# Attention with a relative bias and a squared-relu FFN on one core: the order of every engine's instructions taken from a list scheduler

## The chip, the cores and the metric

The kernel runs on one core of a Trainium2 chip. The metric is the device time of one execution in microseconds (us), the median over several runs. A core has five engines that each work through a list of instructions in order: TensorE (PE in the profile, with its weight loads shown apart as PEld), VectorE (DVE), ScalarE (ACT), GpSimd (POOL, which here issues DMAs and sets memory) and SyncE (SP, which here issues DMAs). An engine waits at an instruction until what it reads has been written and what it writes over has been read; instructions behind it on the same engine wait with it.

## The reference

The inputs are q, k and v with 8 batches, 8 heads, 576 positions and 64 values a head, a bias table of 32 buckets by 8 heads, and FFN weights of 512 x 2048 and 2048 x 512, all fp32. What is computed:

```
scores = scale * np.matmul(q, k.transpose(0, 1, 3, 2))
bias = bias_table[bucket]                  # bucket depends on |i - j| alone
scores = scores + bias.transpose(2, 0, 1)[None, :, :, :]
attn = np.exp(scores - max); attn = attn / (attn.sum + 1e-09)
x = (attn @ v), heads side by side         # 4608 tokens x 512
h = np.maximum(x @ w_in, 0.0)
out = h * h @ w_out                        # 4608 x 512, fp32
```

## The kernel before

The work is cut into 64 *units*. A unit is one pair of heads (two heads side by side fill 128 partitions) with half of a batch's queries, 288 of them. Four units, one a pair of heads, make a *half* h (16 of them, two a batch): 288 tokens with all eight heads, which the FFN can then take.

A unit has five score steps jt over blocks of 128 keys (the fifth has the 64 last keys of both heads). Each is one or two matmuls (`scores`, L264 and L280) into one of two PSUM buffers `st`, an exp on ACT into `et` or `em` (L273, L282), and, where the block touches the band in which the bias changes, a multiply on DVE by the exponentiated bias table `tb_sb` or `tm_sb` (L288). Outside the band the bias is a constant, which drops out in the quotient. Then `pv` (L318) multiplies by v, whose tile `vz` also holds columns of ones, so that the same matmul gives the row sums; each head's result has one PSUM bank. ACT takes Ln of both sums and Exp of minus that (L325, L326, L329), and two multiplies on DVE write the normalised result to `xt` (L335).

For a half that is complete, `ffn1` makes 16 groups of four matmuls (L362) into one PSUM bank `f1` (`hps`), each followed by a relu on ACT into `rt` (L371) and a square on DVE into `g_sb` (L372). `ffn2` makes, per 128 tokens, 16 matmuls of 512 columns (L384) into one bank `f2` (`yps`), a scaled copy on DVE (L390) and a store from SP. `ffn1` of a half needs all eight `xt` multiplies of that half.

q and k must lie transposed. For batches 0 and 1 PE does that (`transposes`, L233, into `f1` or `f2`) and DVE copies the result into `kz` (L250 to L252) and `qt` (L246). From batch 2 on, POOL's DMAs write fp16 copies of q and k to DRAM (`halve`), SP's transposing DMAs read them back (`turn`, L157), and DVE spreads k (L160 to L162).

The bias table is made on the chip at the start: exp of the table's differences, one matmul with a constant, a copy on DVE (L202), one DMA to DRAM (`t_bias`) and five DMAs back, in which each partition reads the row shifted by one. All six are on SP. The loads of q, k, v and the weights are on POOL.

What sets the order is written out by hand. `run(h)` lists the slots of a half: score steps, transposes, and the two parts of the `pv` of the unit before at fixed places. After every slot it calls `feed`, which emits `ffn1` groups and pairs of `ffn2` matmuls that are due by a clock of its own: a half lasts STEP = 28 ticks, spread evenly over its slots, `ffn1` of a half begins 9 ticks after the half, and `ffn2` begins at a tick in the third half after it. `defer` and `tick` put the Exp and the two multiplies one slot apart. After the last slot, `alone = True`: the groups of `ffn1` that are left use `f1` and the two `pv` banks by turns, and `ffn2` the score buffers.

Of the kernel before, what the change touches and what calls it, by code (L numbers as in the profile page):

```python
# [21 lines left out]
NBK = 32  # L22
# [8 lines left out]


STEP, AFTER1, AFTER2 = 28, 9, 3

F2_GAP = 4.0

DMA_FROM = 2
F2_PACE = STEP * 16 / 288
F2_START = 5 * STEP + AFTER1 + AFTER2 - 48 * F2_PACE
TILES = [(0, 1), (2, 3), (4, 5), (6, 7, 8)]  # L40
BAND = [(0, 256), (0, 384), (128, 512), (256, 576), (384, 576)]


def _bucket(n):
# [7 lines left out]
    return np.where(n < half, n, large).astype(np.int64)  # L52


@with_exitstack
def kernel(
# [30 lines left out]
    et_pool = ctx.enter_context(tc.tile_pool(name="et", bufs=11))  # L87
    nr_pool = ctx.enter_context(tc.tile_pool(name="nr", bufs=2))
    kt_pool = ctx.enter_context(tc.tile_pool(name="kt", bufs=2))
    em_pool = ctx.enter_context(tc.tile_pool(name="em", bufs=3))  # L90
    xt_pool = ctx.enter_context(tc.tile_pool(name="xt", bufs=2))
    rt_pool = ctx.enter_context(tc.tile_pool(name="rt", bufs=3))
# [22 lines left out]


    def sdma(eng, out_, in_):
        io(eng.dma_start(out=out_, in_=in_))  # L118

    qts, spreads = {}, []  # L120

    def load_qk(b, h0, n):

        for dst, src in zip(h16s[b], (q, k)):
            sdma(
                nc.gpsimd,
                dst[:, h0 : h0 + n, :],
                src[b, h0 : h0 + n].rearrange("h (p t) d -> p h (t d)", t=TPP),
            )

    def halve(b):

        for ic in range(2):
            sdma(
                nc.gpsimd,
                bass.AP(
                    tensor=d16[0],
                    offset=(b * S + ic * IC) * H * D,
                    ap=[[D, H], [H * D, IC], [1, D]],
                ),  # L140
                bass.AP(
                    tensor=q.tensor,
                    offset=q.offset + (b * H * S + (ic + 1) * IC - 1) * D,
                    ap=[[S * D, H], [-D, IC], [1, D]],
                ),
            )
        for h in range(H):
            sdma(nc.gpsimd, d16[1].ap()[b, :, ts(h, D)], k[b, h])

    def turn(p):  # L150

        b, hp = divmod(p, 4)
        qt = qt_pool.tile([128, S], FP16, tag="qt", name="qt")
        kz = kzs[p % 5]
        kt = kt_pool.tile([128, S], FP16, tag="kt", name="kt")
        for out_, src in ((qt, d16[0]), (kt, d16[1])):
            io(nc.sync.dma_start_transpose(out=out_, in_=src.ap()[b, :, ts(hp, 128)]))  # L157
# [424 lines left out]
```

## Time and profile before

| what | value |
|---|---|
| time, median of 3 runs (lowest, highest) | 473.96 us (473.86, 474.88) |
| the profiled execution's own time | 472.76 us |
| its span, first to last instruction | 470.9 us |
| mean clock granted to TensorE | 0.976 |
| PE, ACT, DVE, POOL busy | 429.9, 338.2, 271.5, 125.3 us |
| first `hps` matmul, first `yps` matmul begin at | 42.0, 77.5 us |
| last scores' exp ends, last `yps` matmul begins | 427.4, 466.3 us |
| DMA moved | 36.58 MB |

The profile is one execution. A row of a group names the line, the engine, the operation and the tiles, with its count, its busy time and the mean of one; behind the second bar stands how long the engine was idle just before and what ended that. A row of the timeline has start, length, engine, line and count, and in square brackets the idle time before it and its releaser. A row of waits has the total, the number and the longest. Since matmuls overlap, a busy PE is not a PE at its peak.

### The profile page before, as it was taken

How to read it: one execution, taken by the hardware profiler on the slowest of the kernel's cores; microseconds unless marked ns; L12 is line 12 of the kernel's file. 1: busy time of each engine (PE TensorE's matmuls, PEld its weight loads, DVE VectorE, ACT ScalarE, POOL GpSimd, SP SyncE). 2: the span in 40 equal slices, each digit the busy share in tenths (PEclk: the TensorE clock that was granted, in tenths of full speed). 3: DMA queues.
4: the chain of work that ended last, by engine and by line, in shares of the span. 5: the costliest groups of instructions: out<-in, count | busy, mean ns of one | idle time of the engine just before them, and what ended most of it. 6: DMA issues, size and time to landing. Idle time of an engine off the chain costs nothing.

```text
span 470.9 us, 8483 instructions
## 1 busy us (share of the span) xinstructions
PE 429.9 (91%) x3023; PEld 282.5 (60%) x3023; DVE 271.5 (58%) x790; ACT 338.2 (72%) x770; POOL 125.3 (27%) x169
## 2 busy tenths in 40 slices
PE   6477988999999999999999999999999999996996
PEld 2244656666666666666666666666666666663552
DVE  5768955565555755556556655565556655553331
ACT  2287888787778877787778877787778877784330
POOL 7948285003800084003800084003200000000000
PEclk9599999999999999999999999999999999998899
DMA  9999999543994289344994189433514200000011
GB/s 125 205 200 129 149 98 95 70 86 44 90 112 67 61 73 119 75 62 56 92 112 75 53 71 120 75 69 48 52 49 61 61 24 24 22 24 23 24 45 67
DMA packets 165801, 36.58 MB, mean 78 GB/s; under 512 B 152920, under 2 KB 161152, under 8 KB 165760
## 3 DMA queue, kind: packets, MB, share of 16 engines
q0 software_dynamic: 129504, 18.47, 53.7%
q1 hardware_dynamic: 36256, 17.59, 16.0%
q8 instruction: 23, 0.38, 0.4%
q14 instruction: 18, 0.15, 0.1%
HBM read 37.75 MB, written 16.52 MB: 115 GB/s over the span
## 4 chain that ended last, share of the span: by engine, by line
PE 78%; ACT 10%; DVE 6%; issue 3%; DMA 3%; SPq 0%; DVEq 0%
PE yps L384 26%; PE hps L362 24%; PE pv L318 14%; PE st L264 12%; ACT et L273 4%; ACT rt L371 2%; ACT r L326 2%; ACT r L325 1%; DMA t_bias<-tv_sb 1%; PE st L280 1%; DVE xt L335 1%; DMA tb_sb<-t_bias 1%; DVE kz L251 1%; DVE kz L250 1%; DVE y L390 1%
## 5 line engine op out<-in xcount | busy, mean ns | idle before, releaser
L273 ACT ACTIVATE et<-st 128x576 f16<-128x576 f32 x256 | 164.1, 645 | 24.1 <-PE st L264 22.6
L362 PE MATMUL hps<-xt,w_in_sb 128*128 128x288 f16 x1024 | 168.1, 287 | 5.4 <-ACT rt L371 3.5
L384 PE MATMUL yps<-w_out_sb,g_sb 128*128 128x512 f16 x576 | 167.1, 381 | 0.6 <-DVE y L390 0.6
L371 ACT ACTIVATE rt<-hps 128x288 f16<-128x288 f32 x256 | 104.6, 409 | 80.5 <-PE hps L362 80.3
L288 DVE TENSOR_TENSOR et<-et,tb_sb 128x512 f16<-128x512 f16 (+3 forms) x224 | 79.2, 356 | 111.3 <-ACT et L273 105.2
L362 PEld LDWEIGHTS <-w_in_sb 128*128 128x128 f16 x1024 | 100.2, 98 | 55.1 <-issue 6.7
L264 PE MATMUL st<-qt,kz 128*128 128x288 f16 x512 | 104.8, 288 | 18.3 <-ACT et L273 14.7
L372 DVE TENSOR_TENSOR g_sb<-rt 128x288 f16<-128x288 f16 x256 | 78.5, 307 | 58.9 <-ACT rt L371 55.7
L118 POOL DMA_DIRECT2D vz<-in_v_dram x80 | 57.9, 739 | 174.7 <-PE pv L318 163.1
L318 PE MATMUL pv<-et,vz 128*128 128x288 f16 x512 | 84.6, 289 | 1.0 <-DVE xt L335 1.0
L264 PEld LDWEIGHTS <-kz 128*128 128x128 f16 x512 | 49.7, 98 | 58.7 <-issue 27.1
L318 PEld LDWEIGHTS <-vz 128*128 128x128 f16 x640 | 62.7, 99 | 26.6 <-DVE xt L335 1.4
L384 PEld LDWEIGHTS <-g_sb 128*128 128x128 f16 x576 | 56.6, 98 | 22.4 <-issue 1.7
L335 DVE TENSOR_TENSOR xt<-pv,r 64x288 f16<-64x288 f32 x128 | 58.0, 453 | 4.7 <-ACT r L329 1.9
L118 POOL DMA_DIRECT2D k<-in_k_dram x48 | 30.9, 680 | 31.1 <-DMA q<-in_q_dram 23.6
L318 PE MATMUL pv<-em,vz 128*128 128x288 f16 x128 | 36.9, 288 | 1.1 <-DVE em L288 1.1
L390 DVE TENSOR_SCALAR y<-yps 128x512 f32<-128x512 f32 x36 | 24.9, 692 | 11.7 <-PE yps L384 11.0
L329 ACT ACTIVATE r<-r 128x288 f32<-128x288 f32 x64 | 28.3, 443 | 2.0
L325 ACT ACTIVATE r<-pv 64x288 f32<-64x288 f32 x64 | 26.1, 407 | 4.9 <-PE pv L318 3.5
L326 ACT ACTIVATE r<-pv 64x288 f32<-64x288 f32 x64 | 25.8, 402 | 4.2 <-PE pv L318 2.6
L282 ACT ACTIVATE em<-st 128x288 f16<-128x288 f32 x64 | 26.3, 411 | 0.0
L118 POOL DMA_DIRECT2D q<-in_q_dram x12 | 21.3, 1804 | 0.0
(42 smaller groups left out, 115.3 us busy)
## 6 DMA issues: line engine op xcount, KB each, us to landing
out_dram<-y SPq DMA_DIRECT2D x36, 256.0 KB, 2.2
vz<-in_v_dram POOLq DMA_DIRECT2D x64, 64.0 KB, 3.0
q<-in_q_dram POOLq DMA_DIRECT2D x12, 288.0 KB, 9.8
k<-in_k_dram POOLq DMA_DIRECT2D x48, 72.0 KB, 8.4
w_in_sb<-in_moe_w_in_dram POOLq DMA_DIRECT2D x4, 512.0 KB, 11.3
w_out_sb<-in_moe_w_out_dram POOLq DMA_DIRECT2D x4, 512.0 KB, 9.1
qh<-in_q_dram POOLq DMA_DIRECT2D x3, 288.0 KB, 9.9
kh<-in_k_dram POOLq DMA_DIRECT2D x3, 288.0 KB, 10.7
```

What stands on the lines that cost most here:

```text
L118: io(eng.dma_start(out=out_, in_=in_))
L264: nc.tensor.matmul(st[:, e, 0:IC], kz[:, ds(640 * e + jt * 128, 128)], qt[:, ds(c0, IC)], start=True, stop=True,)
L273: io(nc.scalar.activation(out=et, in_=st[:, :, 0:IC], func=EXPF, scale=SCALE))
L288: io(nc.vector.tensor_tensor(out=sl, in0=sl, in1=tab, op=MULT))
L318: nc.tensor.matmul(pvs[e][:, 0:IC], vz[:, jt, 2 * hp + e, :], rhs, start=(jt == 0), stop=(jt == 4))
L325: io(nc.scalar.activation(out=r[0:64, :], in_=pvs[0][64:128, 0:IC], func=LNF))
L326: io(nc.scalar.activation(out=r[64:128, :], in_=pvs[1][0:64, 0:IC], func=LNF))
L335: nc.vector.tensor_tensor(out=xt[o : o + 64, hp, ds(ic * IC, IC)][:, ::-1], in0=pvs[e][o : o + 64, 0:IC], in1=r[o : o + 64, :], op=MULT,)
L362: nc.tensor.matmul(hps[:, 0:IC], w_in_sb[:, kk, ts(nt, 128)], xt[:, kk, ds(h % 2 * IC, IC)], start=(kk == 0), stop=(kk == 3),)
L371: io(nc.scalar.activation(out=rt, in_=hps[:, 0:IC], func=RELUF))
L372: io(nc.vector.tensor_tensor(out=g_sb[:, nt, o : o + IC], in0=rt, in1=rt, op=MULT))
L384: nc.tensor.matmul(yps, g_sb[:, nt, ts(m, 128)], w_out_sb[:, nt, :], start=(nt == 0), stop=(nt == 15))
```

## The change

All instructions are first recorded as operations of a plan, each with its engine, a stream on that engine, how long it occupies the engine, how long until its result can be used, and the operations that it depends on (those that write what it reads, and those that must be done with a buffer before it is used again). Within a stream the order is that of recording; between the streams of an engine it is free. The plan then runs a list schedule over all engines with those modelled times: of each engine it takes the head that can start first, on PE among heads that can start within 0.02 us the one with the earliest due time, and then the earliest over all engines. What comes out is the order in which the kernel emits its instructions. At run time nothing of it is left but the order. The fixed slots, `feed`, `defer` and their constants go.

Other edits: the table's write and its reads move from SP to POOL, into the sequence of the loads, with the two reads of the first four heads made one; q and k of heads 4 to 7 of batch 0 are loaded two heads at a time; three of the five zero fills of `kz` become ACT copies of the first; pair 0's copy of q goes from DVE to ACT; the warm-up matmuls go from 14 to 11; pair 1, 2 and 3 are transposed one unit ahead instead of by written places; the `pv` banks are lent to `ffn1` in the last half only, where before all groups that were left used them.

The core of the diff (the tiles and the arithmetic of each operation are as before):

```diff
-STEP, AFTER1, AFTER2 = 28, 9, 3
-F2_GAP = 4.0
+P, T0 = 6.25, 8.0
...
+class Plan:
+    def run(self):
+        free = dict.fromkeys(self.streams, 0.0)
+        dma = 0.0
+        while any(q for x in self.streams.values() for q in x.values()):
+            best = None
+            for eng, x in self.streams.items():
+                heads = []
+                for q in x.values():
+                    if q and all(d.at is not None for d in q[0].deps):
+                        ready = max([d.done for d in q[0].deps], default=0.0)
+                        heads.append((max(free[eng], ready), ready, q))
+                if not heads:
+                    continue
+                first = min(h[0] for h in heads)
+                if eng == "PE":
+                    at, _, q = min((h for h in heads if h[0] <= first + 0.02), key=lambda h: h[2][0].due)
+                else:
+                    at, _, q = min(heads, key=lambda h: (h[0], h[1]))
+                if best is None or at < best[0]:
+                    best = (at, eng, q)
+            at, eng, q = best
+            o = q.popleft()
+            o.at, o.done = at, at + o.lat
+            free[eng] = at + o.occ
+            if o.load:
+                dma = max(dma, at + o.occ) + o.load
+                o.done = dma + 2.0
+            self.order.append(o)
+        return self.order
...
-    sdma(nc.sync, tdram.ap(), tv_sb)
+    loads_v[0] = load_v(0, 0, vz_set[0])
+    written = pool(tdram.ap(), tv_sb, 0.1, [tv])
+    loads_v[0] += load_v(0, 1, vz_set[0])
...
+    tbs = [table_read(0, 4)] * 2
+    loads_qk[0, 4] = loads_qk[0, 5] = load_qk(0, 4, 2)
+    loads_v[0] += [x for h in range(2, 4) for x in load_v(0, h)]
+    loads_qk[0, 6] = loads_qk[0, 7] = load_qk(0, 6, 2)
+    tbs += [table_read(4, 4)] * 2
+    loads_v[0] += [x for h in range(4, 8) for x in load_v(0, h)]
+    tms = [table_mixed(e) for e in range(2)]
+    w_ins, w_outs, halves = [load_w_in(0)], [], {}
...
+        e_op = add("ACT", "exp", 0.557 if two else 0.31, 0.72 if two else 0.48, s_exp, [s_op, *war])
...
+            mults[n].append(add("DVE", "mult", 0.39, 0.52, mult(e), [x] + free))
...
+            tag = ("f1", "p0", "p1")[nt % 3] if h == 2 * B - 1 else "f1"
...
+            m = add(
+                "PE",
+                "f1",
+                0.49,
+                0.71,
+                mm,
+                [x for i in range(4) for x in mults[4 * h + i]] + [before, w_ins[nt // 4]],
+                T0 + P * (4 * (h + 1) + 2.2 + nt / 4),
+            )
+            f1_ops[h].append(m)
+            r = add("ACT", "relu", 0.33, 0.47, relu, [m, sq_all[-RT] if len(sq_all) >= RT else None])
...
+                    add(
+                        "PE",
+                        "f2",
+                        0.432,
+                        0.64,
+                        mm(k2),
+                        deps + (before if k2 == 0 else []),
+                        T0 + P * (12 + (8 * j + k2) * 64 / 288),
+                    )
...
+    for o in plan.run():
+        o.fn()
```

What moves, at three places. The first is DVE after the zero fills, at the first two pairs of heads (`kz0` and `kz1` are the k tiles of pairs 0 and 1, `qt` a pair's q, `et` an exp with its band multiply). Before:

```order
L250 COPY kz0_106<-tp_168 64x576
L251 COPY kz0_106<-tp_168 64x576
L252 COPY kz0_106<-kz0_106 64x64
L246 COPY qt_197<-tp_184 128x576
L288 TENSOR_TENSOR et_227<-et_227,tb_sb_94 128x2x256
L288 TENSOR_TENSOR et_233<-et_233,tb_sb_94 128x576
L250 COPY kz1_107<-tp_236 64x576
L251 COPY kz1_107<-tp_236 64x576
L252 COPY kz1_107<-kz1_107 64x64
L246 COPY qt_265<-tp_252 128x576
```

With the change:

```order
L433 COPY kz0_106<-tp_150 64x576
L439 COPY kz0_106<-tp_150 64x576
L447 COPY kz0_106<-kz0_106 64x64
L433 COPY kz1_107<-tp_185 64x576
L439 COPY kz1_107<-tp_185 64x576
L447 COPY kz1_107<-kz1_107 64x64
L425 COPY qt_230<-tp_199 128x576
L530 TENSOR_TENSOR et_220<-et_220,tb_sb_94 128x2x256
L530 TENSOR_TENSOR et_224<-et_224,tb_sb_94 128x576
```

The copies of pair 1 have moved ahead of the first two band multiplies, and pair 0's copy of q is gone from DVE.

The second is POOL after the loads of heads 0 to 3. Before (the table's DMAs are on SP):

```order
L118 DMA qh0_102<-in_q_dram 96x4x384
L118 DMA kh0_103<-in_k_dram 96x4x384
L118 DMA vz0_111<-in_v_dram 128x4x64
L118 DMA vz0_111<-in_v_dram 64x4x64
L118 DMA vz0_111<-in_v_dram 128x4x64 x6
L118 DMA w_in_sb_92<-in_moe_w_in_dram 128x4x512
```

With the change:

```order
L174 DMA vz0_111<-in_v_dram 128x4x64
L174 DMA vz0_111<-in_v_dram 64x4x64
L174 DMA t_bias<-tv_sb_99 8x512
L174 DMA vz0_111<-in_v_dram 128x4x64
L174 DMA vz0_111<-in_v_dram 64x4x64
L174 DMA tb_sb_94<-t_bias 128x4x384
L174 DMA qh0_102<-in_q_dram 96x2x384
L174 DMA kh0_103<-in_k_dram 96x2x384
L174 DMA vz0_111<-in_v_dram 128x4x64 x2
```

The table's write and its first read stand ahead of q and k of heads 4 to 7, and the weights follow behind all of them.

The third is ACT at the last unit (`em` is its last exp, the three `r` its Ln, Ln and Exp, `rt` the relus of the FFN). Before:

```order
L273 ACTIVATE et_6124<-st_6121 128x576
L371 ACTIVATE rt_6134<-hps_6129 128x288
L282 ACTIVATE em_6144<-st_6142 128x288
L325 ACTIVATE r_6159<-pv0_6147 64x288
L326 ACTIVATE r_6159<-pv1_6148 64x288
L329 ACTIVATE r_6159<-r_6159 128x288
L371 ACTIVATE rt_6170<-hps_6165 128x288
```

With the change:

```order
L649 ACTIVATE rt_6090<-hps_6079 128x288
L515 ACTIVATE em_6095<-st_6088 128x288
L649 ACTIVATE rt_6109<-hps_6100 128x288
L569 ACTIVATE r_6123<-pv0_6111 64x288
L649 ACTIVATE rt_6127<-hps_6118 128x288
L569 ACTIVATE r_6123<-pv1_6129 64x288
L616 ACTIVATE r_6123<-r_6123 128x288
L649 ACTIVATE rt_6147<-hps_6136 128x288
```

Relus, and with them groups of the FFN on PE, now stand between the steps of the last unit, where before none stood.

More of the change, by code (lines that the diff above doesn't have):

```diff
@@ L415, in feed @@
[L415 to L423 removed]
+            loads.append(pool(d16[1].ap()[b, :, ts(h, D)], k[b, h], 1.3))
+        return loads
     tabs = list(hw_specs.get_activation_tables(nc.m.arch))
```

825 lines of the change are left out of this document (471 added, 354 removed).

## Prediction

> **What bounds the kernel now.** I read the page first, then the run cut into four stretches (stage windows), then what TensorE waited for, then the chain of waits at the start.
>
> ```profile
> span 470.9 us, 8483 instructions
> PE 429.9 (91%) x3023; PEld 282.5 (60%) x3023; DVE 271.5 (58%) x790; ACT 338.2 (72%) x770; POOL 125.3 (27%) x169
> PE 78%; ACT 10%; DVE 6%; issue 3%; DMA 3%; SPq 0%; DVEq 0%
> ```
>
> PE holds 78% of the chain. What an order can change is the rest, so I need PE's own demand. Matmuls overlap, so I take start to start: four `hps` matmuls begin at 455.23 and the next at 455.72, and the last 50 `yps` take 10.96 us.
>
> ```profile
> 455.23 0.65 PE L362 MATMUL hps<-xt,w_in_sb 128*128 128x288 f16 x4
> 455.72 10.96 PE L384 MATMUL yps<-w_out_sb,g_sb 128*128 128x512 f16 x50
> 36.16 0.45 PE L233 MATMUL tp<-id_sb,kh 96*64 96x96 f16 x12
> 36.54 0.66 PE L318 MATMUL pv<-et,vz 128*128 128x288 f16 x4
> ```
>
> That is 0.49/4 = 0.122 us for 288 columns and (10.96-0.38)/49 = 0.216 us for 512. Twelve transposes take 0.38 us, 0.032 each. The program has 576 `st`, 640 `pv` and 1024 `hps` of 288 columns (2240 x 0.122 = 273.3), 576 `yps` (124.4) and 192 transposes (6.1): 403.8 us. So 67 us of the span are not demand. Where they lie:
>
> ```profile
> 0.00:41.95 41.95, 25.18 (x226) 14.50 (x227) 27.54 (x58) 20.94 (x41) 30.07 (x49) 0.84 1.27 162
> 41.95:68.10 26.15, 23.14 (x226) 16.12 (x224) 21.33 (x55) 21.75 (x51) 15.11 (x20) 1.00 1.56 140
> 68.10:427.90 359.80, 346.36 (x2386) 232.62 (x2383) 209.25 (x643) 285.50 (x656) 80.10 (x102) 1.00 0.64 67
> 427.90:470.90 43.00, 35.21 (x190) 19.27 (x190) 13.39 (x35) 10.03 (x25) 0.00 (x0) 0.90 0.11 43
> ```
>
> (Window, length, then busy us and count of PE, weight loads, DVE, ACT, POOL, then PE's clock and DMA.) By 68.1 PE has done 242 matmuls of 288 columns and its 192 transposes, 29.5+6.1 = 35.6 us of demand: 32.5 lost. From there to 427.9, 2386 matmuls, 480 of them `yps`: 1906 x 0.122 + 480 x 0.216 = 336.2 of 359.8, so 23.6 lost. At the end 94 x 0.122 + 96 x 0.216 = 32.2 of 43.0: 10.8 lost, 4.6 of it after the last matmul (466.3). The sum closes: 32.5+23.6+10.8 = 66.9.
>
> **The start.** The chain begins with the bias table:
>
> ```profile
> 5.60 5.14 DMA t_bias<-tv_sb
> 10.76 3.96 DMA tb_sb<-t_bias
> 14.82 0.79 DVE et L288 x2
> 15.62 0.66 DVE kz L250
> 18.76 0.77 DVE qt L246
> 20.26 0.61 PE st L264 x2
> 10.15 2.57 ACT L273 ACTIVATE et<-st 128x576 f16<-128x576 f32 x4 [6.23 <-PE st L264]
> ```
>
> DVE stands at the first band multiply until 14.82. Pair 1's copies (from 15.62 to 19.5) are queued behind it, and the scores that need them begin at 20.26. In the new order pair 1's copies stand ahead of the first band, so that wait holds only bands and the `pv` after them. One zero fill leaves DVE and two leave POOL for ACT, and pair 0's q copy goes to ACT: ACT stood idle 6.23 us before its first exp, which hides them; without that cover they would push the first exp back by their own length, some 2 us (an estimate from the DVE copy of 0.76 and fills of its size). The table still has to go out and come back: I put the first band at 13.8, one microsecond earlier, since its write and reads no longer share DMA with loads issued after them.
>
> From there DVE sets the pace until all eight pairs are transposed. Rows of DVE up to the last `qt` copy, which stands just ahead of the first `yps`, counted in the new order: 10 bands of 576, 6 each of 512, 320 and 64, 4 each of 192, 448 and `em`; 6 pairs of copies; 16 `xt`; 13 squares.
>
> ```profile
> L288 DVE TENSOR_TENSOR et<-et,tb_sb 128x576 f16<-128x576 f16 x64 | 29.3, 457 | 48.9 <-ACT et L273 48.4
> L288 DVE TENSOR_TENSOR et<-et,tb_sb 128x512 f16<-128x512 f16 x32 | 13.5, 421 | 5.4 <-DMA tb_sb<-t_bias 5.2
> L251 DVE COPY kz<-tp 64x576 f16<-64x576 f16 x8 | 6.1, 761 | 0.1
> L250 DVE COPY kz<-tp 64x576 f16<-64x576 f16 x8 | 6.0, 748 | 1.0 <-PE tp L233 0.9
> L246 DVE COPY qt<-tp 128x576 f16<-128x576 f16 x8 | 6.1, 758 | 0.6 <-PE tp L233 0.4
> L252 DVE COPY kz<-kz 64x64 f16<-64x64 f16 x8 | 3.5, 441 | 0.3
> L335 DVE TENSOR_TENSOR xt<-pv,r 64x288 f16<-64x288 f32 x128 | 58.0, 453 | 4.7 <-ACT r L329 1.9
> L372 DVE TENSOR_TENSOR g_sb<-rt 128x288 f16<-128x288 f16 x256 | 78.5, 307 | 58.9 <-ACT rt L371 55.7
> L273 ACT ACTIVATE et<-st 128x576 f16<-128x576 f32 x256 | 164.1, 645 | 24.1 <-PE st L264 22.6
> L371 ACT ACTIVATE rt<-hps 128x288 f16<-128x288 f32 x256 | 104.6, 409 | 80.5 <-PE hps L362 80.3
> ```
>
> Copies 6 x (0.748+0.761+0.441+0.758) = 16.2; `xt` 7.2; squares 4.0; bands 13.8 (the four narrow forms, not quoted, scale down to 0.19). Sum 41.2: 13.8 + 41.2 = 55.0 with DVE never idle and nothing overlapped. ACT up to the same place: 41 exps (26.4), 13 relus (5.3), 37 small ones at about 0.41 (15.3): 47.1 from about 9, so 56. The two agree; successive instructions overlap by under 0.1 us (three exps took 1.79, not 1.94), which pays for some idle time. I take **55 for the first `yps`**. At that place the new PE order has done 94 `st`, 90 `pv`, 56 `hps` and all transposes, 240 matmuls against the 242 that the old one reached at 68.1. Start term: **-13.1**, bounds -18 (overlap pays all waits) and -9 (four more of idle).
>
> The filler of those gaps is `yps`, so the loads must be there: the last `w_out_sb` is issued at 41.2 and lands within 11.9, by 53.1.
>
> ```profile
> L118 POOL DMA_DIRECT2D w_out_sb<-in_moe_w_out_dram x4: 772/788/797, 39.0 to 41.2; - x4
> DMA to landing us min/median/max: 6.0/9.1/11.9
> SPq L118 <- DMA t_bias<-tv_sb: 4.8, 1, 4.8
> ```
>
> The table's write and reads now stand in POOL's queue. The 4.8 us that SP waited cost only the table; on POOL q/k of heads 4 to 7, v and every weight stand behind that wait. POOL still issues until about 7.5, and what it has issued takes DMA to about 9, so I charge 2 us to the later loads and nothing to the sum: 53.1 + 2 is 55. The Trainium skill, "DMA: Bandwidth & Descriptors", section "Two DMAs through the same engine are not ordered", says that a DMA reading what another wrote needs a wait on the issuing engine, whatever queue both share. By that rule sharing the queue saves no wait, and the row above agrees that one is taken; it speaks for the third rival.
>
> **The middle.** PE's waits between 68.1 and 427.9:
>
> ```profile
> PE st L264 <- ACT et L273: 8.7, 14, 0.9
> PE hps L362 <- ACT rt L371: 2.9, 11, 0.3
> 415.06 0.65 PE L362 MATMUL hps<-xt,w_in_sb 128*128 128x288 f16 x4
> 415.75 0.41 ACT L371 ACTIVATE rt<-hps 128x288 f16<-128x288 f32 x1 [0.27 <-PE hps L362]
> 416.21 0.65 PE L362 MATMUL hps<-xt,w_in_sb 128*128 128x288 f16 x4 [0.25 <-ACT rt L371]
> ```
>
> They are hand-overs through single or double PSUM buffers, 11.6 us as shown; a modelled end hides the drain, so start to start they make most of the 23.6. The fixed slots put `hps` 1.15 us after `hps` (415.06 to 416.21) whether or not the relu is through. The new order puts another matmul there when its model says that the relu is not. The model's hand-over is 0.71+0.47 = 1.18 against these 1.15, and its exp pitch 0.557 against (1.79-0.645)/2 = 0.57, so it errs little where PE waits; on DVE it is short (0.39 for an `xt` of 0.453). ACT has 74.3 us idle in 359.8, DVE 150, so the filler's hand-overs can be met. The transposing loads and the outputs on SP, and v and the halved q and k on POOL, keep their queues and are issued as their inputs come ready: I cost that at nothing, since they are for the next batch; one that came late would stall DVE's `kz` copies and the scores of a whole batch behind them. Nothing here prices a planned order; the bounds are 4 (group changes alone) and 23.6 (nothing gained). I take the middle, rounded down since the model's two prices fit: 11, so **-12.6**.
>
> **The end.**
>
> ```profile
> 428.47 0.66 PE L318 MATMUL pv<-et,vz 128*128 128x288 f16 x4 [1.02 <-DVE xt L335]
> 430.18 0.28 PE L318 MATMUL pv<-em,vz 128*128 128x288 f16 x1 [1.05 <-DVE em L288]
> 433.03 2.10 PE L362 MATMUL hps<-xt,w_in_sb 128*128 128x288 f16 x8 [1.95 <-DVE xt L335]
> 430.00:438.00 8.00, 5.87 (x23) 2.97 (x23) 1.97 (x6) 2.49 (x6) 0.00 (x0) 0.58 0.09 33
> ```
>
> PE stands three times because everything after the last scores uses the `pv` banks, and then runs at clock 0.58. The new order keeps 29 `hps` of the half before and 24 `yps` (8.7 us) between the last `pv` and the first `hps` that needs it, against a chain Ln, Ln, Exp, two multiplies of 430.79 to 433.03. So 10.8-4.6 = 6.2 falls to 2 (bounds 0.5 and 6.2): **-4.2**. The Trainium skill, "TensorE: Matmul & The Clock Gate", Part 1, puts the half clock down to idle windows of about 3.4 us; the row agrees (2.2 us empty, then slow), and without that gap the slow stretch should go too.
>
> **The sum.** The profiled execution took 472.76, 1.9 around its span; the runs' median, 473.96, lies 1.2 above that. 470.9 - 13.1 - 12.6 - 4.2 = 441.0 of span, 442.9 profiled, **444** as a median. The builder's work is done before launch; the three warm-up matmuls dropped and 11 instead of 14 cost nothing, since PE has no other work then.
>
> **The rivals.**
> 1. *Hand-overs stay late* in the middle: the written order is static, and each `xt` 0.06 longer than modelled moves what follows. The 23.6 stay: 444+12.6 = **457**. For it: DVE rows; against: the 1.15.
> 2. *Better than half*: start -18, middle 4: 444-5-7 = **432**.
> 3. *The queue's wait holds the loads*: the full 4.8 falls on the weights, 53.1+4.8 = 58, and q/k of heads 4 to 7 stall DVE 2 more: first `yps` at 60, **449**. For it: the row of SP's wait; against: DMA has issued work to drain meanwhile.
> 4. *Slower*: `hps` has one buffer, and the planned order starts each group at the modelled end of its relu. If the chip's ACT is an exp late there, every one of 256 groups stalls; at 0.2 us each that is 51 us instead of 11: **484**. It decides from (11+30)/256 = 0.16 us a group. Against: 1.15 measured, and a stall gives ACT time to catch up.
> 5. *Not what it says*: the start's gain is given back, since PE is bound from 68 on anyway and `w_out` moves late: **474**. Against: the demand of 403.8 leaves room everywhere.
>
> **How the numbers follow.** Forecast 0.58 (own range 435 to 453), rivals in turn 0.12, 0.09, 0.12, 0.07, 0.02. The range 431 to 460 takes in the forecast, the first and third rival and most of the second; the fourth and fifth lie outside. Faster by over 0.2% (0.95 us, about what these runs tell from nothing): 0.58+0.12+0.09+0.12 = 0.91; within 0.02; slower 0.07.
>
> **What would show it.** First `hps` near 30 and first `yps` near 55 (start); PE's waits on `et` and `rt` under half of 11.6 (middle); no idle above 1 us and clock 1.0 after the last `pv` (end). A first `yps` after 60, or `hps <- rt` above 20 us, would make the forecast wrong.

## The result and the profile after

The changed kernel takes **436.93 us** (median of 4 runs, 436.44 to 439.16) against 474.09 (473.86 to 474.88) for the kernel before on the same chip: ratio 0.922, 95% interval 0.919 to 0.926. The profiled execution took 437.1 us, with a span of 435.3. The forecast was 444 (431 to 460), faster with a chance of 0.91.

The head of the page of the changed kernel, and its chain of waits by engine:

```profile
span 435.3 us, 8549 instructions
PE 422.0 (97%) x3020; PEld 283.1 (65%) x3020; DVE 276.1 (63%) x788; ACT 341.7 (79%) x774; POOL 128.9 (30%) x174
PE 90%; DVE 4%; ACT 4%; issue 1%; DMA 1%; SPq 0%; DVEq 0%
```

PE now holds 90% of the chain instead of 78%, with the same work. To see where the 35.6 us of span came from, I cut both runs where PE has begun the same amount of its demand (at 0.122, 0.216 and 0.032 us a matmul, as in the prediction): 35.4 us of it, which is the first `yps` of the changed kernel, and 371.8 us, which leaves 32.0 of work. Those places are at 67.85 and 428.73 us before. Columns: window, its length, then busy us and count of PE, weight loads, DVE, ACT and POOL, PE's clock, DMA's share and GB/s. The kernel before:

```profile
0.00:67.85 67.85, 48.06 (x448) 30.42 (x448) 48.77 (x113) 42.43 (x91) 44.93 (x68) 0.90 1.38 154
67.85:428.73 360.88, 346.87 (x2391) 233.03 (x2389) 210.11 (x646) 285.89 (x656) 80.35 (x102) 1.00 0.64 67
428.73:470.90 42.17, 34.95 (x190) 19.06 (x187) 12.62 (x33) 9.89 (x24) 0.00 (x0) 0.89 0.12 44
```

The changed kernel, cut at the same work:

```profile
0.00:59.90 59.90, 50.88 (x444) 31.22 (x445) 45.27 (x110) 46.33 (x98) 41.05 (x62) 1.00 1.23 155
59.90:398.70 338.80, 338.67 (x2390) 233.75 (x2390) 218.19 (x647) 285.91 (x654) 87.80 (x112) 1.00 0.73 75
398.70:435.30 36.60, 32.43 (x187) 18.08 (x185) 12.65 (x32) 9.50 (x24) 0.00 (x0) 0.98 0.13 51
```

The start is 8.0 us shorter (forecast 13.1), the middle 22.1 (forecast 12.6), the end 5.6 (forecast 4.2). The middle's demand is 371.8-35.4 = 336.4, so it lost 24.5 us before and loses 2.4 now. The end needs 32.0. From the start of the last matmul to the end of the span 4.6 us pass before and 4.1 now (431.25 to 435.32), so the end lost 42.2-32.0-4.6 = 5.6 us before and loses 0.5 now.

**The start**, in rows of the timeline of the changed kernel: the table, the first multiply with the band (with six that follow), the first `hps`, the first `yps`.

```profile
9.68 0.77 POOL L174 DMA_DIRECT2D tb_sb<-t_bias  x1 [1.77 <-DMA t_bias<-tv_sb]
14.71 2.07 DVE L530 TENSOR_TENSOR et<-et,tb_sb 128x512 f16<-128x512 f16 x7 [2.56 <-ACT et L512]
35.78 0.41 PE L638 MATMUL hps<-xt,w_in_sb 128*128 128x288 f16 x2
59.90 0.59 PE L696 MATMUL yps<-w_out_sb,g_sb 128*128 128x512 f16 x2
```

POOL waits 1.77 us for the table's write, where SP waited 4.8. The row of the band names ACT as what ended DVE's wait, but the two exps that begin at 10.68 were through by 11.9. What ended it is the read of the table: issued at 9.68, it landed at 14.62. So the band still begins at 14.71 (before 14.82), `hps` 6.2 us earlier than before, not 12.

**The middle**: PE's waits over the whole run of the changed kernel (total, number, longest), and a piece of its timeline.

```profile
PE st L497 <- ACT et L512: 3.4, 8, 0.9
PE hps L638 <- ACT rt L649: 1.1, 3, 0.5
PE pv L556 <- DVE xt L582: 0.8, 2, 0.5
```

```profile
232.09 0.65 PE L638 MATMUL hps<-xt,w_in_sb 128*128 128x288 f16 x4
232.58 0.41 PE L497 MATMUL st<-qt,kz 128*128 128x288 f16 x2
232.78 0.41 ACT L649 ACTIVATE rt<-hps 128x288 f16<-128x288 f32 x1 [0.19 <-PE hps L638]
232.83 0.59 PE L696 MATMUL yps<-w_out_sb,g_sb 128*128 128x512 f16 x2
233.26 0.65 PE L638 MATMUL hps<-xt,w_in_sb 128*128 128x288 f16 x4
```

The waits on `et` stand in the start; from 68.1 to 398.7 us the trace shows no wait of PE. The relu of the `hps` from 232.09 is through at 233.19, and PE fills that time with one `st` and one pair of `yps`: 0.49+0.25+0.43 = 1.17 us from `hps` to `hps`, hardly more than `hps` and relu take. Where a `pv` is ready, it stands there instead.

A measure that needs no pitch: how many matmuls PE begins in the same 290 us, from 100 to 390. First the kernel before, then the changed one.

```profile
100.00:390.00 290.00, 280.63 (x1930) 188.24 (x1929) 171.72 (x532) 229.48 (x526) 69.84 (x89) 1.00 0.68 73
```

```profile
100.00:390.00 290.00, 289.87 (x2043) 199.63 (x2042) 186.52 (x554) 244.08 (x557) 66.05 (x84) 1.00 0.63 71
```

5.9% more matmuls in the same time.

**The end** of the changed kernel has one wait after the last `pv`, and the clock is 1.00 up to the last stores:

```profile
400.36 0.65 PE L638 MATMUL hps<-xt,w_in_sb 128*128 128x288 f16 x4 [0.50 <-ACT rt L649]
419.81 11.82 PE L696 MATMUL yps<-w_out_sb,g_sb 128*128 128x512 f16 x54
```

### The profile page after: what moved, and what is told of

Its sections match the earlier page's. It is cut to its first block, busy times and chain, and to the rows that moved or that the text cites. A ratio compares the mean times of both kernels' runs of the same rounds, so it can differ in the third digit from the quotient of the medians.

```text
span 435.3 us, 8549 instructions
## 1 busy us (share of the span) xinstructions
PE 422.0 (97%) x3020; PEld 283.1 (65%) x3020; DVE 276.1 (63%) x788; ACT 341.7 (79%) x774; POOL 128.9 (30%) x174
## 3 DMA queue, kind: packets, MB, share of 16 engines
q0 software_dynamic: 129888, 19.46, 58.6%
## 4 chain that ended last, share of the span: by engine, by line
PE 90%; DVE 4%; ACT 4%; issue 1%; DMA 1%; SPq 0%; DVEq 0%
PE yps L696 28%; PE hps L638 28%; PE pv L556 17%; PE st L497 15%; ACT et L512 2%; PE tp L398 1%; ACT r L569 1%; DVE kz L433 1%; DVE et L530 1%; DMA oh_sb<-c_oh 1%; DVE xt L582 1%; PE warm L295 1%; DVE kz L439 1%; ACT r L616 1%; DVE qt L425 0%
## 5 line engine op out<-in xcount | busy, mean ns | idle before, releaser
L696 PE MATMUL yps<-w_out_sb,g_sb 128*128 128x512 f16 x576 | 164.4, 379 | 0.3
L649 ACT ACTIVATE rt<-hps 128x288 f16<-128x288 f32 x256 | 104.4, 408 | 40.0 <-PE hps L638 37.5
L497 PE MATMUL st<-qt,kz 128*128 128x288 f16 x576 | 117.3, 290 | 5.3 <-ACT et L512 3.4
L530 DVE TENSOR_TENSOR et<-et,tb_sb 128x512 f16<-128x512 f16 (+3 forms) x224 | 77.8, 356 | 39.3 <-ACT et L512 38.1
L497 PEld LDWEIGHTS <-kz 128*128 128x128 f16 x576 | 56.3, 99 | 37.1 <-issue 6.0
L709 DVE TENSOR_SCALAR y<-yps 128x512 f32<-128x512 f32 x36 | 24.9, 691 | 14.0 <-PE yps L696 13.1
L476 DVE COPY kz<-kt 64x576 f16<-64x576 f16 (+2 forms) x72 | 18.2, 280 | 1.5 <-DMA kt<-k 1.2
```

Source lines behind the costliest of these rows:

```text
L497: io(nc.tensor.matmul(st[:, e, 0:IC], kz[:, c : c + 128], qts[p][:, ds(c0, IC)], start=True, stop=True))
L530: io(nc.vector.tensor_tensor(out=sl, in0=sl, in1=tab, op=MULT))
L649: io(nc.scalar.activation(out=rts[h, nt], in_=hpt[h, nt][:, 0:IC], func=RELUF))
L696: nc.tensor.matmul(ypt[j], g_sb[:, nt, ts(m, 128)], w_out_sb[:, nt, :], start=(nt == 0), stop=(nt == 15),)
```

## The experiments

All kernels but the one with the banks alone start from the changed kernel. Where a time, a dependence or a queue of the plan is edited, the whole order is planned anew. A *stand* is a time in which an engine waits. The table gives the median of the timed runs, and for the profiled execution where PE has begun 35.4 us of its demand, how long it took from there to 371.8 us of it, and what was left of the span. The last row has no cuts, since PE has less to do there. The cuts are of one execution each. With `yps` held it took 440.7 us (median 443.2), with ACT x 1.2 467.9 (463.5), with no band and the table on SP 438.1 (435.3), with batch 1 by DMA 451.7 (454.7); the others lie within 2 us of their medians.

| kernel | median us | 35.4 reached at | from there to 371.8 | rest of the span |
|---|---|---|---|---|
| before | 474.1 | 67.9 | 360.9 | 42.2 |
| changed | 436.9 | 59.9 | 338.8 | 36.6 |
| banks at the end only (from before) | 471.4 | 69.6 | 360.8 | 39.0 |
| due before ready | 465.8 | 59.4 | 367.9 | 37.5 |
| ACT modelled x 0.8 | 445.0 | 59.1 | 347.4 | 36.7 |
| ACT modelled x 1.1 | 447.7 | 59.2 | 344.6 | 40.4 |
| ACT modelled x 1.2 | 463.5 | 60.3 | 365.5 | 40.3 |
| times as measured | 443.6 | 60.2 | 345.8 | 36.6 |
| first `yps` held | 443.2 | 58.6 | 343.8 | 36.6 |
| table on SP | 436.7 | 60.0 | 338.3 | 37.2 |
| start, ACT less | 436.5 | 58.6 | 340.3 | 36.6 |
| start, DVE less | 436.7 | 58.6 | 339.5 | 36.7 |
| no band, table on SP | 435.3 | 60.8 | 338.3 | 37.3 |
| batch 1 by DMA | 454.7 | - | - | - |

### The middle: what makes PE full

**Does taking ready work make it?** One number of the scheduler: how far ahead of the first that could start PE may look for an earlier due time.

```diff
-at, _, q = min((h for h in heads if h[0] <= first + 0.02), key=lambda h: h[2][0].due)
+at, _, q = min((h for h in heads if h[0] <= first + 2.0), key=lambda h: h[2][0].due)
```

> The changed kernel with one number of the scheduler changed: PE takes the operation with the earliest due time among those that could start within 2.0 us of the first one, instead of within 0.02 us. So PE may be planned to wait for a due operation instead of taking one that is ready. Theory A (the middle's gain comes from taking ready work in the place of a late hand-over): the middle falls back by most of its 22 us, 452 to 462 us, PE's waits on et and rt well above 4 us. Theory B (the gain is in the table of due times, and PE would find work either way): 437 to 442 us.

465.75 us (ratio to before 0.981, 0.977 to 0.984). The middle loses 31.5 us, more than before the change: theory A's mechanism, above its range. Waits of PE, and its 290 us:

```profile
PE hps L638 <- ACT rt L649: 11.9, 51, 0.5
PE yps L696 <- DVE y L709: 7.2, 12, 3.7
```

```profile
100.00:390.00 290.00, 280.14 (x1916) 187.62 (x1915) 175.19 (x522) 231.65 (x523) 69.85 (x89) 0.99 0.65 70
```

The same scheduler, the same modelled times and the same due times fall back below the hand-written order's 1930 matmuls once PE may be planned to wait. So the due times alone do not bring the middle's gain; it needs PE to take what is ready. Whether taking what is ready would do without the due times, and what the new orders of DVE and ACT bring by themselves, no run shows. Of the 29.1 us by which the middle is longer than in the changed kernel, 7.6 lie between 60 and 80 us of demand, where a copy waits for a late DMA (see the truer model below).

**How exact must the model be?** Every modelled time of ACT is scaled, by 0.8 as shown, by 1.2 and by 1.1; the instructions stay the same.

```diff
     def add(self, eng, stream, occ, lat, fn, deps=(), due=0.0, load=0.0):
+        if eng == "ACT":
+            occ, lat = 0.8 * occ, 0.8 * lat
```

> The changed kernel with every modelled time of ACT multiplied by 0.8 in the scheduler (the instructions are the same, only the order built from the model differs). Theory A (the order has slack at the hand-overs, the model need not be exact): 437 to 441 us, PE's waits on et and rt together below 10 us. Theory B (the fourth rival of the prediction: the order starts each group at the modelled end of its relu or exp; modelled 0.1 us early, each of 256 groups stalls by about that): 455 to 465 us, PE's waits on rt above 15 us.

> The changed kernel with every modelled time of ACT multiplied by 1.2 in the scheduler (only the order differs). Theory A (slack on either side): 437 to 441 us. Theory B (a model on the cautious side puts more between hand-overs and costs nothing in the middle, but spreads the start, where ACT is modelled as the slow engine): first yps 1 to 3 us later, 438 to 441 us. Theory C (order quality depends on the model within 20%): above 445 us.

> The changed kernel with every modelled time of ACT multiplied by 1.1 (1.2 took 463.5 us, 0.8 took 445.0; only the order differs). Theory A (a threshold: at 1.2 the modelled ACT, 324 us of occupancy times 1.2, no longer fits beside the modelled PE and the planner takes ACT for the bound; at 1.1 it still fits): 437 to 442 us. Theory B (each hand-over pays in proportion to the error): about half of the 26.6 us, 448 to 453 us.

Measured 444.99 (ratio 0.939, 0.936 to 0.941), 463.53 (0.979, 0.974 to 0.984) and 447.74 (0.943, 0.940 to 0.946): 8.1, 26.6 and 10.8 us above the changed kernel. The second has theory C's size; the first lies between its two theories, and the third just below theory B. The short model cost a third of what the fourth rival's 0.1 us a group would make, the order has no slack for 20% either way, and the threshold that theory A of the third expected falls: 10% long already costs 11 us. The kernel with 1.2 begins 1932 matmuls in its 290 us, as many as before the change, and waits:

```profile
PE yps L698 <- DVE g_sb L655: 7.5, 2, 5.7
PE hps L640 <- ACT rt L651: 7.1, 19, 0.5
PE pv L558 <- DVE xt L584: 5.2, 14, 0.8
```

```profile
100.00:390.00 290.00, 280.84 (x1932) 188.38 (x1930) 175.96 (x531) 232.28 (x531) 69.87 (x89) 1.00 0.65 70
```

In the row of `yps` 5.7 us are one stand at a late DMA: between 60 and 80 us of demand this execution loses 8.7 us against the changed kernel. The rest is spread over the run. The start times of `hps` groups go with it: between 150 and 350 us, 39 of the 127 steps from group to group are 1.15 to 1.25 us in the changed kernel, and none in the one with 1.2, where 27 of 120 are near 1.4. I read this as follows, though all of ACT's times were scaled and the relu's alone was not tried: a relu believed to be longer puts more work between two groups than the chip needs, groups pile up behind, and PE later has nothing else. With 1.1 the end pays too, 3.8 us: six `hps` at 398.6 to 418.3 wait 0.50 us each, of which two rows are

```profile
398.62 0.65 PE L640 MATMUL hps<-xt,w_in_sb 128*128 128x288 f16 x4 [0.50 <-ACT rt L651]
415.95 0.65 PE L640 MATMUL hps<-xt,w_in_sb 128*128 128x288 f16 x4 [0.50 <-ACT rt L651]
```

**Is a truer model better?** The times of DVE, ACT and the halving DMAs are set to what the changed kernel's own trace shows back to back.

```diff
-mults[n].append(add("DVE", "mult", 0.39, 0.52, mult(e), [x] + free))
+mults[n].append(add("DVE", "mult", 0.48, 0.61, mult(e), [x] + free))
...
-                    6.0,
+                    3.2,
```

(The second pair of lines is the DMA time of a halved q. Likewise the copies of `kz` and the transposes, Ln, relu, the single exp, and k's 1.3 to 0.5.)

> The changed kernel with the scheduler's times brought to those of its own trace, back to back: the xt multiply 0.48 us instead of 0.39, the spreading copies of kz 0.31, 0.28 and 0.18 instead of 0.22, 0.22 and 0.15, the copies of transposes 0.76 and 0.79 instead of 0.68 and 0.70, the logarithm 0.43 instead of 0.40, the relu 0.31 instead of 0.33, and the halved q and k 3.2 and 0.5 us of DMA instead of 6.0 and 1.3. Theory A (the middle has only 2.4 us to lose and the start hangs on loads and on the ring of engines, not on these times): 435.5 to 438 us. Theory B (the short times of DVE cost the start and the hand-overs, as the first rival of the prediction had it): 430 to 434 us. Theory C (a few per cent of model in the wrong place upset the order as 20% do): above 440 us.

443.62 us (ratio 0.934, 0.931 to 0.938), 6.7 us worse: the size of theory C, but not its mechanism. From 100 us on this order is as full as the changed kernel's, 2045 matmuls against 2043. Its loss lies in one place:

```profile
91.29 0.70 DVE L476 COPY kz<-kt 64x576 f16<-64x576 f16 x3 [5.15 <-DMA kt<-k]
94.59 1.01 PE L696 MATMUL yps<-w_out_sb,g_sb 128*128 128x512 f16 x2 [4.38 <-DVE y L709]
```

```profile
100.00:390.00 290.00, 289.94 (x2045) 199.98 (x2044) 186.40 (x551) 243.82 (x559) 69.86 (x89) 1.00 0.65 72
```

DVE's order has a copy of batch 2's k where the transposing DMA has not landed; the `y` copy stands behind it on DVE, and PE behind that, because `yps` has one bank. PE's clock, 0.92 from 89 to 94.5 us, is then 0.50 from 94.5 to 100, so that between 60 and 80 us of demand this kernel loses 7.0 us against the changed one, with a stand of 4.38. Which of the times I changed moved the copy was not separated. Nearly the same stand of DVE is in other kernels: 6.56 us at 92.85 with ACT x 1.2, 5.03 at 92.00 with due before ready. In the changed kernel DVE's three such waits sum to 1.2 us and PE has none: it passes this place with almost nothing to spare.

### The start: what keeps the first `yps` at 59.9

**The table's queue.** The write of the table and, by a like edit, its four reads go back to SP. The plan then takes the loads of heads 4 to 7 for earlier, so the orders of PE, DVE and ACT differ too, from 12 to 17 us on.

```diff
-    written = pool(tdram.ap(), tv_sb, 0.1, [tv])
+    written = on_sp(tdram.ap(), tv_sb, 0.1, [tv])
```

> The changed kernel with one part undone: the table's write and its two reads go back from POOL's queue to SP's; the order of everything else is built in the same way. Theory A (the queue is worth little: in the changed kernel the first band multiply stands at 14.71 us against 14.82 before, so the wait only changed its place): 435 to 439 us, first band within 0.7 us of 14.71, first yps within 1 us of 59.9. Theory B (the third rival of the prediction: the wait of 1.77 us on POOL holds the loads behind it and is what kept the first yps at 59.9 rather than 55): loads land 1.5 to 2 us earlier, first yps at 57 to 58, 434 to 435 us. Theory C (one queue by need does shorten the start, since on SP the table's reads share DMA with loads issued ahead of them): first band at 16 or later, 438 to 440 us.

436.69 us (ratio 0.921, 0.918 to 0.924), the same as the changed kernel. Theory A has the total and the first `yps`, not the band; the two others have their mechanism, in the two rows:

```profile
11.90 0.69 PE L401 MATMUL tp<-id_sb,kh 96*64 96x96 f16 x12
15.69 1.47 DVE L533 TENSOR_TENSOR et<-et,tb_sb 128x512 f16<-128x512 f16 x5 [0.34 <-DMA tb_sb<-t_bias]
```

Pair 2's transposes begin 4.7 us earlier (16.61 in the changed kernel), since its loads no longer stand behind POOL's wait (k of heads 4 and 5 lands at 11.28 instead of 16.04) and the plan counts on that; the band begins 1.0 us later. Pair 3's k lands at 18.41 in both. The first `yps` stands at 60.0.

**One engine less.** In the first kernel the Exp of the normaliser is left out for the first eight units, in the second the 16 multiplies with the band of the first half. The order of the rest is kept.

```diff
-lambda: io(nc.scalar.activation(out=rs[n], in_=rs[n], func=EXPF, scale=-1.0)),
+lambda: None if n < 8 else io(nc.scalar.activation(out=rs[n], in_=rs[n], func=EXPF, scale=-1.0)),
```

> The changed kernel, order kept, with work left out: the Exp of the normaliser (L616) is not issued for the first eight units, so the outputs of batch 0 are not those of the reference. ACT has 8 instructions of about 0.41 us less before 60 us, 3.3 us. Theory A (ACT's stream sets the start): first yps about 3 us earlier, 433 to 434.5 us. Theory B (DVE sets it): within 0.7 us of 59.9, 436 to 437.5 us. Theory C (the two hand work to each other, neither alone is the bound): between, 1 to 2 us earlier.

```diff
             def band():
+                if n < 4:
+                    return
```

> The changed kernel, order kept, with work left out: the 16 multiplies with the band in the first half of batch 0 are not issued, so those outputs are not those of the reference. DVE has about 5.6 us less before 50 us, and the wait for the table at 14.7 us moves to a later multiply. Theory A (DVE's stream sets the start): first yps 4 to 6 us earlier, 431 to 433 us. Theory B (ACT sets it): within 0.7 us of 59.9, 436 to 437.5 us. Theory C (each waits for the other): 1 to 3 us earlier, 434 to 436 us.

436.48 us (ratio 0.920, 0.918 to 0.923) and 436.74 (0.921, 0.918 to 0.924); the first `yps` at 58.6 in both. That looks like 1.3 us, but the kernel with `yps` held (below), whose order is the changed kernel's up to there, reached the same work at 58.6 too: the starts of profiled executions with one order differ by that much. So taking 3.5 us from ACT (the eight Exps in the changed kernel's trace), or 5.1 us from DVE (its busy time falls from 276.1 to 271.0), moved the start by nothing that can be told from this spread. By the total theory B holds in both, so neither engine alone sets the start. In the second kernel DVE, with no band to do, stands for pair 2's loads instead:

```profile
16.27 0.69 PE L398 MATMUL tp<-id_sb,kh 96*64 96x96 f16 x12 [2.08 <-DMA kh<-in_k_dram]
17.00 0.75 DVE L433 COPY kz<-tp 64x576 f16<-64x576 f16 x1 [5.41 <-PE tp L398]
```

**Both at once.** The bands left out and the table on SP.

> Two edits of the earlier runs together: the table's write and reads on SP's queue (heads 4 and 5 then land at 11.3 us instead of 16.0) and the 16 multiplies with the band in the first half of batch 0 left out (so those outputs are not those of the reference, and DVE has 5.6 us less). Alone, neither moved the start: with the table on SP the first band stood at 15.7 us, and without the bands pair 2's transposes stood for the loads until 16.3 us. Theory A (the two waits cover each other): pair 2's transposes by 13 us, first yps 56 to 57 us. Theory B (a ring of PE, ACT and DVE sets the pace after 20 us, whatever happened before): first yps 58 to 60 us. For the time: 435 to 437 us by both, since PE stood at the second batch's copies when the start was 1.3 us shorter.

435.31 us (434.0 to 438.1; ratio 0.916, 0.913 to 0.919). Pair 2's transposes begin at 11.29, as theory A had it, and still the first 35.4 us of work take 60.8 in the execution that was profiled, about theory B's end. That execution is the slowest of five; where the others, up to 4.1 us shorter, gain, no trace shows, so theory A is not ruled out for them. In this one the next loads are in the way:

```profile
20.07 0.69 PE L401 MATMUL tp<-id_sb,kh 96*64 96x96 f16 x12 [2.66 <-DMA kh<-in_k_dram]
```

In pieces of PE's demand, the times from 10 to 20 us of it and from 20 to 35.4 are nearly the same whatever was taken out: 14.8 and 18.1 in the changed kernel, 14.5 and 18.0 with less on ACT, 14.8 and 18.1 with less on DVE, 14.3 and 17.9 with both edits (15.9 and 19.7 before). The first 10 us of work end at 27.0 in the changed kernel and between 25.7 and 28.6 in these; before at 32.3.

**The first `yps` held** until the place it had before.

```diff
-deps + (before if k2 == 0 else []),
+deps + (before if k2 == 0 else []) + (f1_ops[1][7:8] if h == 0 and k2 == 0 else []),
```

> The changed kernel with one added dependence: the first yps may not start before 32 of the feed-forward groups of the half after the first one are issued, about the place it had in the old order. Theory A (after the start PE is full, so what counts is how early PE has other work than the scores; the start's gain comes from order of bands and copies and this filler matters little): 437 to 439 us. Theory B (the yps are the filler of the gaps between 60 and 70 us; without them PE stands there as it did before): 440 to 443 us, with PE's loss before 75 us up by 3 to 6 us.

443.24 us (ratio 0.935, 0.930 to 0.940): theory B, 6.3 us worse. In the profiled execution it takes 27.7 us from 35.4 to 60 us of work instead of 25.0; another 2.6 us are lost at 124.34, where the shifted order has DVE stand 5.33 us for `kt<-k`. So the early `yps` are worth about 3 us by themselves as filler.

**Batch 1 through the transposing DMAs**, an attempt to be faster: 96 transposes less on PE, 3.1 us of demand.

```diff
-DMA_FROM = 2
+DMA_FROM = 1
...
+    halves[1] = halve(1)
```

> The changed kernel with q and k of batch 1 transposed by the DMA engines, as those of the later batches are, instead of by 96 TensorE transposes and DVE copies. It takes 96 x 0.032 = 3.1 us of demand from PE and 20 copies of 0.44 to 0.76 us and four fills from DVE's start, and adds its loads to the queues between 10 and 25 us. Theory A (after the start PE is 97% busy, so demand counts in full, and DVE's copies are part of what sets the start): 428 to 433 us, first yps near 55. Theory B (the loads of batch 1's q and k push w_in and w_out later, and the start loses what PE gains): 435 to 440 us. Theory C (the transposed loads come late and batch 1's scores stand): above 440 us.

454.73 us (ratio 0.959, 0.953 to 0.964): theory C. The last transposed k of batch 1 is issued at 54.00 and lands at 66.86, among the loads of `w_out`:

```profile
66.88 0.70 DVE L473 COPY kz<-kt 64x576 f16<-64x576 f16 x3 [8.70 <-DMA kt<-k]
68.80 1.12 PE L553 MATMUL pv<-et,vz 128*128 128x288 f16 x4 [8.62 <-DVE xt L579]
```

PE's clock is 0.50 from there to 72 us.

### The end

**The banks alone**, as an edit of the kernel before: `pv`'s banks are lent in the last half only.

```diff
-            if alone and nt % 3:
+            if h == 2 * B - 1 and nt % 3:
```

> The kernel before with one part of the change alone: the feed-forward groups use the banks of pv only in the last half instead of from the half in which the scores are over. No scheduler, the old fixed order elsewhere. Theory A (the end term of the prediction is right and stands by itself, 4.2 us: the three stands of 1.02, 1.05 and 1.95 us come from the shared banks): 468 to 470.5 us, the clock in the last 43 us back near 1.0. Theory B (it is the order of yps and hps there, not the banks): 473 to 475 us, the same stands in the last 43 us. Theory C (single-buffered hps in the half before costs more than the banks bring, 32 groups at up to 0.5 us): above 475 us.

471.39 us (ratio 0.995, 0.993 to 0.997), faster by 2.7, less than theory A. The rest of the span is 3.2 us shorter, and the clock there is 0.99 instead of 0.89:

```profile
430.41:469.40 38.99, 32.79 (x190) 18.27 (x187) 12.60 (x33) 9.75 (x24) 0.00 (x0) 0.99 0.13 47
```

```profile
430.15 0.66 PE L318 MATMUL pv<-et,vz 128*128 128x288 f16 x4 [1.01 <-DVE xt L335]
431.87 0.28 PE L318 MATMUL pv<-em,vz 128*128 128x288 f16 x1 [1.05 <-DVE em L288]
434.02 0.65 PE L362 MATMUL hps<-xt,w_in_sb 128*128 128x288 f16 x4 [0.77 <-ACT rt L371]
```

The stand of 1.95 us for `xt` is gone; those of 1.01 and 1.05 us stay, so they do not come from the shared banks, to which the prediction put them down. Of the end's 5.6 us the banks bring 3.2; of the other 2.4, 0.6 lie behind the start of the last matmul, where the runs differ by that much (4.7 us with the table on SP, 4.1 in the changed kernel), and 1.8 are left for the new order.

No kernel tried here that does all the work is faster than the changed one by more than the runs can tell.

## Why the prediction was right and where it was wrong

**The total** lay in the range, 7 us under the number, with two steps wrong in opposite directions: 5.1 us too much from the start, 9.5 too little from the middle, 1.4 too little from the end. 441.0+5.1-9.5-1.4 = 435.2 of span, against 435.3 measured. That the first two partly cancel is luck. Start and middle both lie outside their own bounds: -8.0 against -18 to -9, and 2.4 us of loss against 4 to 23.6.

**The demand.** That PE holds the chain, with 403.8 us of demand and 67 us lost, held: the changed kernel loses 435.3-403.8 = 31.5, of which 59.9-35.4 = 24.5 in the start, 2.4 in the middle and 4.6 in the end, 4.1 of these after the last matmul has begun.

**The start** is the step that failed: "DVE sets the pace until all eight pairs are transposed", 13.8 + 41.2 = 55. At 59.9 the first `yps` came only just before the forecast's own sign of being wrong ("after 60"). Its parts: the band came at 14.71, 0.9 late: the read of the table was issued 1.1 us earlier than before, but took 4.94 us to land, not 3.96. It brings four heads instead of two, and from POOL's queue; from SP's the same read took 6.59 (issued 9.01, landed 15.60), so its size alone does not set that time. The 41.2 us of DVE overlap to 37.4, but DVE also waits, and 45.2 pass. The stretch from 14.70 to 59.90 in the changed kernel, and two pieces of it:

```profile
14.70:59.90 45.20, 39.14 (x371) 26.26 (x371) 37.42 (x94) 38.92 (x86) 29.81 (x42) 1.00 1.37 172
```

```profile
45.00:60.00 15.00, 14.17 (x143) 10.04 (x142) 14.07 (x39) 14.01 (x33) 8.05 (x9) 1.00 1.40 167
25.00:35.00 10.00, 7.22 (x56) 4.59 (x57) 6.20 (x17) 9.14 (x20) 6.17 (x12) 1.00 1.28 205
```

DVE is busy 37.4 of 45.2 us, ACT 38.9: neither is full, and taking 5.1 us from the one or 3.5 from the other changed nothing. An engine's busy time is a lower bound; I read the pace as set by different things one after the other. Up to about 20 us the loads of pairs 2 and 3 stand close behind: PE does not wait for them in the changed kernel, but does, 2.08 and 2.66 us, once the bands are left out. In the last 15 us PE, DVE and ACT are each busy 14, so that less work on one leaves the other two. What holds the stretch between 10 and 20 us of PE's work (27 to 42 us), with 4.3 to 4.8 us of loss in every variant, was not found: ACT is busy 9.1 of 10 us between 25 and 35, yet 1.3 us less on it there (the Exps at 29.2, 33.2 and 38.9) gained 0.3.

Nor is it separated which of the edits brings the 8.0 us. 5.3 of them come in the first 10 us of PE's work (32.3 to 27.0); the table's queue brings none, and the copies ahead of the bands, the fills and the copy given to ACT and the loads by pairs were not undone one by one. PE's clock rose with them, from 0.90 to 1.00 over the start. With less on ACT it was 0.50 from 15 to 20 us, and the first `yps` still came at 58.6, so such a stretch does not by itself cost the start; before the change the clock was 0.50 for longer, from 12 to 24.6 us.

**The third rival**, loads behind POOL's wait, gave "first `yps` at 60", and it came at 59.9. The table on SP shows that it is still not the cause: without that wait on POOL it stands at 60.0. The rule cited with it, of the Trainium skill, "DMA: Bandwidth & Descriptors", "Two DMAs through the same engine are not ordered", agrees with the row of 1.77 us: the read waits for the write's landing although both are on POOL. What a read without that wait would find, no run here shows.

**The middle** was taken as 11 us of loss between bounds of 4 and 23.6. It lost 2.4, below the bound: "group changes alone" cost next to nothing, since start to start a change from `hps` to `st` or `yps` keeps the pitch of its columns. The mechanism was right: due before ready shows that the gain needs the taking of ready work, and the 1.15 us of the fixed slots stayed, at 1.17, with the hand-over now filled. "Rounded down since the model's two prices fit" was the right argument, used too timidly: the runs with ACT's times wrong by 10 and 20% lose 6 to 27 us more in the middle, so the prices had to be right within a few per cent to be worth nearly all of it. **The second rival** had such a middle (4 us of loss), but the start the wrong way, at -18.

**The first rival** named `xt`, 0.06 us too short in the model. With 0.48 for it, among the other measured times, PE from 100 us on is as full as with 0.39: on DVE, with idle time to spare, the error cost nothing that shows there. **The fourth rival** has its mechanism (a planned order against a wrong relu), but its price of full stalls at every group was far off: x 0.8 costs 8.1 us in all, and PE's waits on `rt` are 2.9.

**Costed at nothing**, "one that came late would stall DVE's `kz` copies": right for the changed kernel (1.2 us on DVE, none on PE), and the price behind it turned out to be the largest in this order. It decides the truer model, batch 1 by DMA, and part of three others. It also eats what is gained ahead of it: the start with less on ACT is 1.3 us ahead at 60 us of work and 0.2 behind at 80, and in between stand these rows of its timeline, the `y` copy on DVE behind the late k:

```profile
96.91 0.93 DVE L476 COPY kz<-kt 64x576 f16<-64x576 f16 x3 [2.17 <-DMA kt<-k]
100.64 0.69 DVE L709 TENSOR_SCALAR y<-yps 128x512 f32<-128x512 f32 x1
101.38 1.02 PE L696 MATMUL yps<-w_out_sb,g_sb 128*128 128x512 f16 x4 [1.41 <-DVE y L709]
```

**The end** went to its lower bound: 0.5 us lost, in one wait of 0.50, clock 1.00, 5.6 us gained for 4.2. Two of its three stands were put down to the banks wrongly, as said above. The rule of the half clock (the Trainium skill, "TensorE: Matmul & The Clock Gate", Part 1), an idle window of about 3.4 us, agrees with both kernels in direction only. Before, the clock was 1.00 from 428 to 431 us and 0.50 from 431.5 to 438, though the longest stand, from 431.08 to 433.03, is 1.95 us; with the banks alone two stands of 1.0 us stayed and the clock over the end was 0.99. How much idle time it takes, these runs do not show.

## What to carry to other kernels

Where one engine has the demand, price a planned order by what the hand-overs lose now, and expect most of it back (here 22.1 of 24.5 us) if the planner lets that engine take whatever is ready and its prices of the hand-over are right within a few per cent; scale one engine's prices by a tenth to see how far the gain holds. Price a ramp not by the sum of its busiest engine but by all things it waits for in turn, loads among them, and test it by taking work away before moving any. After each change of order look at copies that wait for a DMA: an order plans their landing, nothing makes the landing come then, and everything behind them on that engine waits too.

## What was not expected of the hardware

The transposing DMAs land at very different times. Over the run of the changed kernel their median from issue to landing is 2.7 and 2.8 us; between 60 and 100 us, beside the halving loads, the loads of v and the stores, 9.7 and 7.2. First the whole run, then that window:

```profile
qt<-q SPq DMA_TRANSPOSE x24, 2.7
kt<-k SPq DMA_TRANSPOSE x24, 2.8
```

```profile
q<-in_q_dram POOLq DMA_DIRECT2D x2, 288.0 KB, 10.5
qt<-q SPq DMA_TRANSPOSE x4, 9.7
kt<-k SPq DMA_TRANSPOSE x4, 7.2
```

And a model closer to the measured times gave a slower kernel, by 6.7 us, through one such copy.
